# A copy moved ahead of a cast on ScalarE, and the first batch's tokens loaded in eight transfers of one head

## The chip, the core and the metric

The kernel runs on one core of a Trainium2 chip. The core has a matrix engine (TensorE, PE in the profile), three engines for elementwise work (VectorE or DVE, ScalarE or ACT, GpSimd or POOL) and a sync engine (SyncE or SP) that mostly issues DMA transfers. PE writes its products to PSUM, from which ACT or DVE copies them to SBUF; DMA moves data between main memory (HBM) and SBUF. Each engine runs its own instructions strictly in the order of the program and waits on semaphores for the others.

The metric is the device time of one execution in microseconds (us). Lower is better.

## The reference

A cross attention between 512 tokens and 32 state rows, in both directions, for 8 batches of 8 heads, then a feed-forward block over all 8 x 544 rows:

```python
def _attn_ref(x, state):                    # x (8,8,512,64), state (8,8,32,64)
    scale = 1.0 / np.sqrt(D)
    scores = scale * np.matmul(x, state.transpose(0, 1, 3, 2))
    a = softmax(scores)                     # over the 32 states
    xread = np.matmul(a, state)
    scores2 = scale * np.matmul(state, x.transpose(0, 1, 3, 2))
    a2 = softmax(scores2)                   # over the 512 tokens
    sread = np.matmul(a2, x)
    return np.concatenate([xread, sread], axis=2)

def _moe_ref(x, w_in, w_out):               # x (4352, 512): heads side by side
    h = x @ w_in                            # 512 -> 2048
    g = np.maximum(0.01 * h, h)
    return g @ w_out                        # 2048 -> 512
```

Both softmaxes subtract the maximum and add 1e-9 to the sum; they are shortened here.

## The kernel before

**Products.** For the token rows, attention and the first feed-forward product are joined: `a_m` multiplies a batch's states with `w_in` into a matrix M (2 x 128 rows, 2048 columns) in four column quarters of 512, and `ff1` multiplies the probabilities `aT` with M. So M has four quarters for each batch, each a PE product into PSUM and a copy to SBUF by `m_evict`. The second feed-forward product is `piece` for batch 0 and `Batch.run` for the later ones; the latter saves multiplications with sums of weights (`weights_sum`) and of activations.

**Order.** The program is written out by hand: `tc.manual_schedule` leaves every engine the order in which the code names its instructions. Batches overlap: while batch 0's second product runs, batch 1's scores, softmax and M are made and batch 2's tokens are cast. The steps are in the names: `a0`, `a1`, `a2` are batches 0 to 2.

**Queues.** Transfers issued by SyncE (`nc.sync`) and ScalarE (`nc.scalar`) go through one queue each, those of GpSimd (`nc.gpsimd`) through a third. The issue is itself an instruction of that engine, in order with the rest. POOL issues the weights `w_in` and `w_out`, batch 1's tokens (`x1`) and batch 2's (`load_x(2)`).

**The start.** ACT issues the states of batches 0 and 1 (`st0f`, L63). Batch 0's tokens (1 MB of float32, 8 heads) go to two tiles `xf` of four heads each, in transfers of two heads that alternate between SyncE and ScalarE (L68 to L71). Then ACT loads its function table with a warm exponential (L77) and copies the prepared states (`state01`, L164 and L168). `cast_x0` (L118) turns pairs of heads into bfloat16 in `xb`: pair 0 in one cast, pairs 1 and 2 in halves, pair 3 in halves on DVE and POOL (L883 to L889). PE transposes them (`x0_t`, L785), ACT and DVE copy the result to `xT` (`xt0_evict`, L791), and batch 0's scores follow (`scores0`, L800). Until the tokens are there PE runs products of zeros (`spin`, L142).

**Around the copy that is moved.** In this stretch (L1019 to L1048) ACT has, in order: M quarters 1 and 2 of batch 1 (`m_evict`, L388), the exponential of batch 1 (`a_exp`, L246), the cast of batch 2's first four heads (`cast_x`, L113), M quarter 3 of batch 1 (L388 again, two copies of 128x512), and the two exponentials of batch 1's other direction (`a_exp2`, L296), which read the scores in the PSUM bank `sc`. PE has: M quarter 3's product (L376), products of `piece` (L608), then batch 2's M quarter 0 (`a_m(a2, 0, "sc")`, L1070), which is written into the same bank `sc`, and batch 1's `ff1` (L397). POOL casts heads 4 to 7 of batch 2, and SyncE issues the transpose of batch 2's tokens (`a_xt_dma`, L200) once all eight heads are cast.

Of the kernel before, what the change touches and what calls it, by code (L numbers as in the profile page):

```python
# [10 lines left out]
B, H, S, D = 8, 8, 512, 64  # L11
# [5 lines left out]
NK = H // 2  # L17
# [13 lines left out]
def kernel(  # L31
# [9 lines left out]
    nc = tc.nc  # L41
# [15 lines left out]
    VEC, SCA, POO = nc.vector.tensor_copy, nc.scalar.copy, nc.gpsimd.tensor_copy  # L57
# [7 lines left out]
    )  # L65
    xf = [consts.tile([P, NK, NT * D], FP32, name="xf", tag=f"xf{u}") for u in range(2)]
    xv = x[0].rearrange("h (p t) d -> p h (t d)", t=NT)
    for k in range(NK):  # L68
        (nc.sync, nc.scalar)[k % 2].dma_start(
            xf[k // 2][:, 2 * (k % 2):2 * (k % 2) + 2], xv[:, 2 * k:2 * k + 2]  # L70
        )  # L71

    idle = consts.tile([P, S], BF16, name="idle")
    nc.vector.memset(idle[:], 0.0)
# [37 lines left out]
    def cast_x(b, h0, h1, copy):  # L112
        copy(  # L113
            xs[b][:, :, h0:h1].rearrange("p t h d -> p h t d"),
            xl[b][:, h0:h1].rearrange("p h (t d) -> p h t d", t=NT),
        )
# [68 lines left out]
    def state_t(i):  # L185
        POO(stb[i][:], stf[i][:])
        nc.sync.dma_start_transpose(st_t[i][:], stb[i][:].rearrange("p b q -> p (b q)"))
# [11 lines left out]
    def a_xt_dma(a):  # L199
        nc.sync.dma_start_transpose(  # L200
            a.xT[:].rearrange("p t k q -> p (t k) q"),
            a.xb[:].rearrange("p t h d -> p (t h d)"),
        )

    def st_of(a, g, k):
        rows = slice(D * g, D * (g + 1))
        if a.b == 0:
            return stbd[rows, k, g ^ (k // 2), :]
        t = st1 if a.b == 1 else st_t[0][:, a.b - 2] if a.b < 4 else st_t[1][:, a.b - 4]
        return t[rows, NS * k:NS * (k + 1)]  # L210
# [153 lines left out]
    def a_m(a, c, tag):  # L364
        if a.M is None:
            a.M = mpool.tile([P, 2, DFF], BF16, name="M", tag="M")
        if tag in ("ph", "py", "phpy"):
            pm = [psum.tile([P, DM], FP32, name="pm", tag=t) for t in (tag[:2], tag[-2:])]
            at = [t[:] for t in pm]
        else:  # L370
            pm = psum.tile([P, 2, DM], FP32, name="pm", tag=tag, bufs=1)
            at = [pm[:, g, :] for g in range(2)]
        for k in range(NK):
            for g in range(2):
                v, r = (k // 2, 2 * (k % 2) + (g ^ (k // 2))) if a.b == 0 else (g, k)
                nc.tensor.matmul(  # L376
                    at[v][NS * r:NS * (r + 1)],
                    lhsT=st_of(a, g, k),
                    rhs=w_in_bf[D * g:D * (g + 1), k, DM * c:DM * (c + 1)],
                    start=True, stop=True,  # L380
                )
        return pm

    def m_evict(a, c, pm, copy):
        cols = slice(DM * c, DM * (c + 1))
        if isinstance(pm, list):
            for g in range(2):
                copy(a.M[:, g, cols], pm[g][:])  # L388
        else:
            copy(a.M[:, :, cols], pm[:])  # L390
# [211 lines left out]
    def piece(b, hT, i, jq, bank=None, copy=SCA, part=range(4)):  # L602
        if jq == 0:
            y = ys[b, i] = Y()
            y.py = psum.tile([P, DM], FP32, name="py", tag="py")[:] if bank is None else bank
        y = ys[b, i]
        for j in (4 * jq + v for v in part):
            nc.tensor.matmul(  # L608
                y.py, lhsT=hT[:, j, P * i:P * (i + 1)], rhs=w_out_bf[:, j, :],
                start=(j == 0), stop=(j == 15),  # L610
            )
        if jq == 3 and copy is not None:
            y_store(b, i, copy)

    def y_store(b, i, copy):
        tag, bufs = (f"yo{i - 2}", 1) if (b, i) in ((0, 2), (0, 3)) else ("ysb", 3)
        ysb = ypool.tile([P, DM], FP32, name="ysb", tag=tag, bufs=bufs)
        copy(ysb[:], ys[b, i].py)
        if b == B:
            for bb in range(4):  # L620
                r0 = (4 * i + bb) * SROW + S
                nc.sync.dma_start(out[r0:r0 + NS, :], ysb[NS * bb:NS * (bb + 1), :])
        else:
            nc.sync.dma_start(rows_of(b)[i], ysb[:])
# [13 lines left out]
    def weights_sum(dst, m0=0, m1=NM, eng=None):  # L638
        u, v, op = (
            (B12, B11, ALU.subtract), (B11, tw[2], ALU.subtract),  # L640
            (B22, B12, ALU.add), (tw[1], B21, ALU.add),
        )[dst]
        with nc.allow_low_precision(reason="operands of a product"):
            ms = slice(m0, m1)
            (eng or nc.vector).tensor_tensor(out=tw[dst][:, ms], in0=u[:, ms], in1=v[:, ms], op=op)
# [122 lines left out]
    a0, a1, a2 = att_of[:3]  # L768
# [171 lines left out]
    h0 = hpool.tile([P, 16, S], BF16, name="hT", tag="hT")  # L940
# [67 lines left out]
    for u in range(2):  # L1008
        piece(0, h0, 1 + u, 0, bank=wide[:, 0] if u else None)
        ps = psum.tile([P, NT, 2, P], BF16, name="pxt2", tag="ph")  # L1010
        for t in range(NT):
            for v in range(2):
                h = NK * u + 2 * v
# [16 lines left out]
    weights_sum(2, 0, 4, nc.gpsimd)  # L1030
    weights_sum(1, 0, 4, nc.gpsimd)
    state_t(0)
    cast_x(2, 0, 4, SCA)
    for h in range(NK, H):
        cast_x(2, h, h + 1, POO)
    a_open(a2, 2)
    a_xt_dma(a2)
    for i in (2, 3):
        piece(0, h0, i, 1)
    m_evict(a1, 3, a_m(a1, 3, "ph"), SCA)  # L1040
    for g in range(2):
        a_exp2(a1, g)
    load_x(3, nc.sync)
# [78 lines left out]
    for b in range(2, B):  # L1122
# [16 lines left out]
        for s in range(16):  # L1139
            fast = nxt is None and 4 <= s < 12  # L1140
            if fast:
                n = 1 if s in (7, 11) else 2
                k = PACE[s]
# [192 lines left out]
```

## Time and profile before

The profile is of one execution. The table sets the figures beside each other:

| figure | value |
|---|---|
| median of 3 runs | 201.96 us (201.87 to 202.44) |
| the profiled execution's own time | 202.15 us |
| its span in the profile | 200.4 us |
| PE busy | 194.9 us, 97% of the span |
| DVE, ACT, POOL busy | 160.4, 143.6, 55.5 us |
| DMA packets | 28.01 MB, mean 140 GB/s |
| granted TensorE clock | 1.0 in the whole span |

How the profile is read. The span runs from the first to the last instruction; the execution's own time has some 1.75 us more around it. A row of the groups names line, engine and operation, what is written and read, the shape and count, the busy time with the mean length of one, and the idle time of the engine just before these instructions with what ended most of it. A row of the timeline gives the start, the time covered and the instructions, with the idle time before the first and its releaser in brackets. An engine's name with a q (ACTq, SPq) is its sequencer issuing a transfer. A matmul row is longer than the matmul's own cost, since matmuls are pipelined: the distance between starts is the better measure. The chain of waits follows the work that ended last back through what released each step; a large share there says where the time is, not what would be saved if that step were shorter.

### The profile page before, as it was taken

To read this page: it belongs to the slowest core of one execution; us is meant where nothing else is said; L and a number is where in the kernel's file an instruction comes from. 1 tells how busy PE (TensorE), PEld (TensorE's weight loads), DVE (VectorE), ACT (ScalarE), POOL (GpSimd) and SP (SyncE) were. 2 spreads that over 40 slices of the span, in tenths; PEclk is the share of its full clock that TensorE was granted. 3 is DMA by queue.
4 is the path that set the end of the run, shared out by engine and by line. 5 is a ranking of instruction groups with operands and counts; after the bars stand their busy time and mean duration, and the time that the engine had idled before them with its cause. 6 is when DMAs were issued, how large, how long until landed. Compare 5 with 4: busy or idle time off the path is not lost.

```text
span 200.4 us, 4995 instructions
## 1 busy us (share of the span) xinstructions
PE 194.9 (97%) x2066; PEld 134.6 (67%) x2066; DVE 160.4 (80%) x249; ACT 143.6 (72%) x263; POOL 55.5 (28%) x82
## 2 busy tenths in 40 slices
PE   7999999999999999999999999999999999999993
PEld 2566634346676767766776677666767788799882
DVE  2576689999999989975997499779978977995622
ACT  3388747599877867978697859787878768767710
POOL 8393174690036005200420040100020024004250
PEclk9999999999999999999999999999999999999999
DMA  6999997999672892559424844290025102310035
GB/s 184 229 207 261 241 294 130 225 292 202 143 192 53 248 264 50 98 206 258 96 39 169 270 55 89 105 164 0 0 108 157 29 0 87 125 56 0 0 95 170
DMA packets 39510, 28.01 MB, mean 140 GB/s; under 512 B 25344, under 2 KB 36736, under 8 KB 39488
## 3 DMA queue, kind: packets, MB, share of 16 engines
q1 hardware_dynamic: 33712, 20.35, 39.6%
q0 software_dynamic: 4944, 6.55, 16.0%
q10 hardware_dynamic: 832, 0.79, 1.4%
q8 instruction: 16, 0.26, 0.5%
q14 instruction: 6, 0.05, 0.1%
HBM read 17.30 MB, written 8.91 MB: 131 GB/s over the span
## 4 chain that ended last, share of the span: by engine, by line
PE 80%; DMA 14%; POOL 2%; ACT 2%; issue 0%; DVE 0%; POOLq 0%
PE yq L679 43%; PE ph L397 22%; DMA xl<-in_x_dram 8%; DMA w_in_bf<-in_moe_w_in_dram 5%; PE pf L475 3%; PE pm L376 3%; PE yu L679 3%; PE pl L564 2%; PE psn L342 1%; PE sc L216 1%; PE py L608 1%; PE phw L410 1%; POOL w_in_bf L126 1%; ACT e L296 1%; ACT xb L113 1%; ACT M L388 0%
## 5 line engine op out<-in xcount | busy, mean ns | idle before, releaser
L403 ACT ACTIVATE hT<-ph 128x512 bf16<-128x512 f32 x100 | 58.5, 605 | 17.8 <-PE ph L397 17.3
L397 PE MATMUL ph<-aT,M 128*128 128x512 bf16 x200 | 57.7, 379 | 0.0
L679 PEld LDWEIGHTS <-su 128*128 128x128 bf16 x480 | 45.9, 98 | 14.8 <-DVE su L668 0.8
L679 PEld LDWEIGHTS <-hT 128*128 128x128 bf16 x336 | 32.3, 98 | 14.3 <-issue 2.5
L679 PE MATMUL yq<-tw_xf,su 128*128 128x256 bf16 x224 | 31.5, 273 | 0.0
L679 PE MATMUL yq<-w_out_bf,hT 128*128 128x256 bf16 x224 | 31.0, 273 | 0.0
L113 POOL CAST xb<-xl 128x512 bf16<-128x512 f32 (+1 forms) x24 | 13.8, 614 | 48.4 <-DMA xl<-in_x_dram 48.4
L668 DVE TENSOR_TENSOR su<-hT 128x1024 bf16<-128x1024 bf16 (+1 forms) x27 | 18.9, 703 | 6.7 <-ACT hT L403 6.7
L397 PEld LDWEIGHTS <-M 128*128 128x128 bf16 x200 | 19.5, 98 | 5.7 <-issue 0.2
L751 POOL TENSOR_TENSOR yo<-sv,sv 128x512 f32<-128x512 f32 x7 | 9.2, 1310 | 41.0 <-issue 20.3
L688 ACT COPY sv<-yq 128x512 f32<-128x512 f32 x28 | 16.3, 585 | 3.0 <-PE yq L679 2.5
L679 PE MATMUL yq<-tw_x,su 128*128 128x256 bf16 x112 | 15.5, 273 | 0.0
L679 PE MATMUL yq<-w_out_bf,su 128*128 128x256 bf16 x112 | 15.3, 273 | 0.0
L691 DVE TENSOR_TENSOR yo<-yq,sv 128x512 f32<-128x512 f32 x20 | 13.6, 682 | 1.5 <-PE yq L679 1.5
L679 PE MATMUL yq<-tw_x,hT 128*128 128x256 bf16 x104 | 14.5, 273 | 0.0
L390 ACT CAST M<-pm 128x1024 bf16<-128x1024 f32 x12 | 12.2, 1019 | 0.2 <-PE pm L376 0.2
L296 ACT ACTIVATE e<-sc,mcols 128x512 bf16<-128x512 f32 x16 | 11.0, 694 | 0.6 <-DVE mcols L290 0.6
L608 PEld LDWEIGHTS <-hT 128*128 128x128 bf16 x64 | 5.8, 98 | 7.0 <-issue 1.1
L668 DVE TENSOR_TENSOR su<-su,hT 128x1024 bf16<-128x1024 bf16 x14 | 9.7, 692 | 0.5
L288 DVE TENSOR_REDUCE mcol<-sc 128x2 f32<-128x1024 f32 x8 | 9.7, 1215 | 0.0
L668 DVE TENSOR_TENSOR su<-hT,su 128x2048 bf16<-128x2048 bf16 (+1 forms) x8 | 9.2, 1155 | 0.0
L226 DVE TRANSPOSE_TENSOR_REDUCE mrow<-sc 128x32 f32<-128x1024 f32 x7 | 8.7, 1242 | 0.5 <-PE sc L216 0.5
(173 smaller groups left out, 303.7 us busy)
## 6 DMA issues: line engine op xcount, KB each, us to landing
out_dram<-yo SPq DMA_DIRECT2D x12, 512.0 KB, 2.8
xl<-in_x_dram SPq DMA_DIRECT2D x5, 1024.0 KB, 6.7
w_in_bf<-in_moe_w_in_dram POOLq DMA_DIRECT2D x4, 512.0 KB, 7.8
w_out_bf<-in_moe_w_out_dram POOLq DMA_DIRECT2D x2, 512.0 KB, 12.6
x<-in_x_dram POOLq DMA_DIRECT2D x2, 512.0 KB, 11.5
w_out_bf<-in_moe_w_out_dram POOLq DMA_DIRECT2D x4, 256.0 KB, 13.7
xl<-in_x_dram POOLq DMA_DIRECT2D x1, 1024.0 KB, 16.6
out_dram<-ysb SPq DMA_DIRECT2D x4, 256.0 KB, 5.6
```

The source lines that it names most:

```text
L113: copy(xs[b][:, :, h0:h1].rearrange("p t h d -> p h t d"), xl[b][:, h0:h1].rearrange("p h (t d) -> p h t d", t=NT),)
L226: nc.vector.tensor_reduce(out=m1[:], in_=flat.rearrange("p (c j) -> p c j", j=NS), axis=AX.X, op=ALU.max, apply_transpose=True,)
L288: nc.vector.tensor_reduce(out=m2[:], in_=a.sc[:], axis=AX.X, op=ALU.max, negate=True)
L296: nc.scalar.activation(out=a.e2[:, g], in_=a.sc[:, g, :], func=AF.Exp, bias=a.m2s[:, g:g + 1], scale=SCALE, accum_out=a.r2[:, g:g + 1],)
L390: copy(a.M[:, :, cols], pm[:])
L397: nc.tensor.matmul(ph[:], lhsT=a.M[:, g, P * j:P * (j + 1)], rhs=a.aT[:, g, :], start=(g == 0), stop=(g == 1),)
L403: nc.scalar.activation(out=hT[:, j, :], in_=ph[:], func=AF.Prelu, alpha=0.01)
L668: (eng or nc.vector).tensor_tensor(out=S[n][:, ms], in0=u[:, ms], in1=v[:, ms], op=op)
L679: nc.tensor.matmul(bank[:, i, :], lhsT=lhs[:, m, P * i:P * (i + 1)], rhs=rhs[:, m, :], start=(first and m == 0 and (i == 0 or of is not No ...
L688: copy(t[:], bank)
L691: nc.vector.tensor_tensor(out=dst, in0=bank, in1=self.sv[n][:], op=ALU.add)
L751: nc.gpsimd.tensor_tensor(out=self.yo(1)[:, :, HC:], in0=f.sv[7][:], in1=f.sv[5][:], op=ALU.add)
```

## The change

Two edits, both of order and grouping. Batch 0's tokens are loaded in eight transfers of one head (128 KB) instead of four of two heads, even heads issued by SyncE and odd heads by ScalarE. And the last M quarter of batch 1 (`m_evict(a1, 3, ...)`, with the PE products named before it) stands ahead of batch 2's casts instead of behind them and behind the transpose's issue. What is computed is the same.

```diff
     xv = x[0].rearrange("h (p t) d -> p h (t d)", t=NT)
-    for k in range(NK):
-        (nc.sync, nc.scalar)[k % 2].dma_start(
-            xf[k // 2][:, 2 * (k % 2):2 * (k % 2) + 2], xv[:, 2 * k:2 * k + 2]
-        )
+    for h in range(H):
+        (nc.sync, nc.scalar)[h % 2].dma_start(xf[h // NK][:, h % NK], xv[:, h])
...
     state_t(0)
+    for i in (2, 3):
+        piece(0, h0, i, 1)
+    m_evict(a1, 3, a_m(a1, 3, "ph"), SCA)
     cast_x(2, 0, 4, SCA)
     for h in range(NK, H):
         cast_x(2, h, h + 1, POO)
     a_open(a2, 2)
     a_xt_dma(a2)
-    for i in (2, 3):
-        piece(0, h0, i, 1)
-    m_evict(a1, 3, a_m(a1, 3, "ph"), SCA)
     for g in range(2):
         a_exp2(a1, g)
```

## The prediction

> **What bounds the kernel now.** I read the page first, then the chain of waits, the timelines of TensorE (PE), ScalarE (ACT) and the start, and last the windows of the DMA engines. The page gives PE 97% busy, and its two largest groups of matmuls never wait (last column, idle before them):
>
> ```profile
> L397 PE MATMUL ph<-aT,M 128*128 128x512 bf16 x200 | 57.7, 379 | 0.0
> L679 PE MATMUL yq<-tw_xf,su 128*128 128x256 bf16 x224 | 31.5, 273 | 0.0
> ```
>
> A busy PE is not a full PE, so I checked the pace: four 512-column matmuls take 0.86 us (36.88 to 37.74 in the timeline), 0.216 each, and from 19 us on starts follow each other at that pace. One place breaks it. The timeline of PE (start, length, instructions, count, idle before):
>
> ```profile
> 28.69 1.90 PE L608 MATMUL pyw<-w_out_bf,hT 128*128 128x512 bf16 x8
> 30.52 0.41 PE L376 MATMUL pm<-w_in_bf,st 64*32 64x512 bf16 x8
> 32.60 2.75 PE L608 MATMUL pyw<-w_out_bf,hT 128*128 128x512 bf16 x12
> 35.66 0.41 PE L376 MATMUL pm<-w_in_bf,st_t 64*32 64x512 bf16 x8 [0.31 <-ACT e L296]
> 36.00 1.04 PE L397 MATMUL ph<-aT,M 128*128 128x512 bf16 x4
> ```
>
> The twelve matmuls from 32.60 are through at 32.60 + 12 x 0.216 = 35.19, and the next starts at 35.66: a hole of 0.47 us. The same change from L608 to L376 costs 0.10 where nothing is waited for (28.69 + 8 x 0.216 = 30.42, next start 30.52). So 0.37 us is a wait, and the row names it: L376 wants the PSUM bank "sc", which the two exponentials of batch 1 (L296) still read. ACT at that time:
>
> ```profile
> 30.26 1.06 ACT L246 ACTIVATE e<-sh 128x1024 bf16<-128x1024 f32 x1 [0.37 <-DVE sh L239]
> 32.24 1.04 ACT L113 CAST xb<-xl 128x1024 bf16<-128x1024 f32 x1 [0.93 <-DMA xl<-in_x_dram]
> 33.20 1.06 ACT L388 CAST M<-pm 128x512 bf16<-128x512 f32 x2
> 34.15 0.70 ACT L296 ACTIVATE e<-sc,mcols 128x512 bf16<-128x512 f32 x1
> 35.39 0.22 ACT L296 ACTIVATION_READ_ACCUMULATOR e<-sc,mcols 128x1 f32 x1
> ```
>
> ACT stands still for 0.93 us waiting for batch 2's tokens, while the product that L388 copies (PE at 30.52) has been ready since 30.93. The exponentials end at 35.61, and PE starts 0.05 later.
>
> The start of the kernel, before PE is full:
>
> ```profile
> 0.74 0.42 ACTq L63 DMA_DIRECT2D st0f<-in_state_dram  x1
> 0.75 0.96 SPq L69 DMA_DIRECT2D xf<-in_x_dram  x2
> 1.19 0.98 ACTq L69 DMA_DIRECT2D xf<-in_x_dram  x2
> 2.20 1.28 ACT L77 ACT_TABLE_LOAD   x1 [2.20 <-issue]
> 3.81 0.30 DVE L772 CAST stb<-st0f 128x256 bf16<-128x256 f32 x1 [2.66 <-DMA st0f<-in_state_dram]
> 4.38 0.66 DVE L120 CAST xb<-xf 128x512 bf16<-128x512 f32 x1 [0.27 <-DMA xf<-in_x_dram]
> 6.08 1.12 DVE L120 CAST xb<-xf 128x256 bf16<-128x256 f32 x5 [1.05 <-DMA xf<-in_x_dram]
> 6.94 0.52 POOL L120 CAST xb<-xf 128x256 bf16<-128x256 f32 x1 [1.41 <-DMA xf<-in_x_dram]
> 7.12 1.50 ACT L791 COPY xT<-pxth 128x768 bf16<-128x768 bf16 x2 [1.70 <-PE pxth L785]
> 15.66 0.91 POOL L107 DMA_DIRECT2D xl<-in_x_dram  x1 [0.93 <-DMA w_in_bf<-in_moe_w_in_dram]
> ```
>
> The tile view of xf gives 3.6 to 5.1 us from issue to landing, the view of DMA issues 4.3 as SyncE's median and 5.0 as ScalarE's. With the issues at 0.75 and about 1.2 (SyncE), 1.19 and about 1.7 (ScalarE), the four pairs land at about 4.35, 6.1, 6.3 and 6.8. The five later casts run back to back from the second landing to 7.20; the transposes, ScalarE's copy at 7.12 and the first scores at 7.97 hang on them.
>
> **Part 1, the M quarter moved.** It adds and removes no instruction: two copies of 128x512 (1.06 us together) change places with one cast of 1.04 us. No PE work lies between the old place and the new, and the one transfer between them (the transpose of batch 2's tokens, SyncE) is issued in the same order on its queue. After: exponential L246 until 31.32, the copies at about 31.25 to 32.3 (the product is there at 30.93), in the 0.93 us in which ACT stood still. The cast starts at 32.25 to 32.3 instead of 32.24, at most 0.06 later. Behind it the transpose waits, but it also waits for POOL's last cast, which ends at 33.70 (32.27 + 1.43) against ACT's 33.35, so it is not late. The exponentials then start at 33.2 and end at 34.66 instead of 35.61. PE comes to L376 at 35.19 and finds the bank free: 0.47 becomes 0.10, a gain of **0.37 us**.
>
> What is late next: L376 also needs the transposed states, issued at 31.16 and landing at most 3.8 later, 34.96 (the tile view's longest of two), before 35.29. L397 then starts at 35.63; its aT ends on DVE at 34.76 + 0.69 = 35.45. L216 moves from 38.70 to 38.33; its xT lands at 33.73 + 4.3 = 38.03, and DVE frees "sc" at 36.76 + 1.22 = 37.98. Each holds, by 0.2 to 0.35. DVE is busy without a break from 36 to 44 and does not move up, so these margins are the real bound. Ends for this part: 0 (one of them gives it all back) and -0.37; I take -0.37, as every margin read is positive.
>
> **Part 2, eight transfers.** Bytes, casts and their order stay. SyncE issues 4 instead of 2 at 0.46 us, ScalarE 4 instead of 2 at 0.48, one head each, heads alternating. A cast of a pair of heads now waits for both queues. Mean DMA traffic is 363 to 383 GB/s from 3.0 to 5.5 us (windows), and their sum is 1.11 MB by 5.5; so 1.05 MB of tokens and 0.13 MB of state, moved by about 5.7, stay one stream with one end. The first pair needs the queues' first heads; it may come 0.1 to 0.3 later than 4.35, and the cover is large: PE's idle spins run to 6.0, the cast takes 0.66. The second pair, now third of the five rounds rather than filling ScalarE's queue after the state, may land about 0.4 earlier. The casts behind it are held by pairs three and four, in total bytes where they were.
>
> ScalarE's issues are the cost. The eighth head is the ninth transfer of the SyncE/ScalarE kind. POOL's queue shows what I take to be the rule here: its eleventh to thirteenth issues (15.66, and two of L134 at 17.73 and 20.28) each wait for an earlier POOL transfer to land, the third to the fifth by order, eight before. So I expect head 7's issue to wait for the state's landing, 0.74 + 3.0 = 3.74 by the view of DMA issues, DVE's cast saying 3.8. It is issued 3.85 to 4.33, and queued behind it on ACT are the table load (1.28, to 5.6), the warm exponential (0.20) and two copies (0.53, L164 and L168): done at about 6.4. Next on ACT is L791 at 7.12. The cover is 0.7 us; without it ACT's wait would go straight into the scores.
>
> No row shows such a late issue. From issue to landing the nearest rows give 3.0 (state, same size and queue) and 5.1 (the slowest token pair): head 7 lands between 6.85 and 8.95, where pair four lands at 6.8 now. I take 3.0, as the same size is asked for when the stream is nearly empty: +0.05, and with some 0.05 earlier from pairs two and three the part comes to **0.0**. Its lower end is -0.2: further up, PE's transposes of batch 1 (start 24.56) need a cast that waits for its own transfer and ends at 24.28 whatever the start does. Its upper end is +2.1. A delay there passes to the end whole, since PE is full after it.
>
> **Sum.** The profiled execution took 202.15 us, span 200.4 and 1.75 around it. -0.37 + 0.0 gives a span of 200.0 and 201.8 for that execution. It lies 0.19 above the median of the runs, 201.96; from that, **201.6**.
>
> **Rivals.**
> - *A, as summed*, 201.6, own range 201.4 to 201.8. Chance 0.57.
> - *B, the last head lands behind the weights (slower).* Place: head 7, released at about 3.8, meets the w_in transfers that POOL issues from 3.09 and that fill the engines from 5.5 (windows: 248 GB/s, then 215). For it: the 16 KB state transfers, issued from 20.15 under POOL's traffic, take 5.0 (view of DMA issues). Against it: the state's 3.0. It decides once head 7 lands after about 7.2 (6.85 plus the 0.37 of part 1); at 4.5 from issue it lands at 8.35, +1.5: 203.1. Chance 0.16.
> - *C, the tokens gain too.* Pairs two and three land earlier and the scores with them. For it: DVE idle 1.05 before the casts at 6.08. Against: the last cast needs pair four. At most -0.2 more: 201.4. Chance 0.12.
> - *D, the change does not do what it says.* The hole closes at 35.66 and opens again at aT, xT or "sc", whose margins are 0.2 to 0.35: 202.0. Chance 0.14.
> - *E, transfers of one queue follow each other.* Five of the state's 3.0 on ScalarE's queue end at 0.74 + 15 = 15.7 instead of 6.8, +8.9: 210.5. Against it: ScalarE's two pairs, issued 0.5 apart, land 0.65 apart, and pair two lands 4.9 after its issue behind the state. Chance 0.01.
>
> The Trainium skill (DMA: Bandwidth & Descriptors, Anatomy of one DMA and Rules for kernel authors) speaks against part 2: each transfer carries a fixed cost of some 2 us, small ones should be joined, and several queues share the same engines, which saves issue time only. By that rule, paid in turn, four more transfers on two queues would add 4 us and the sum would be 205.6; the 0.65 between ScalarE's landings bears out the sharing, not the paying in turn.
>
> The skill's same page (Queues, rings and completion order) says that an engine alternates between queues by packets, which would let head 7 in soon after w_in begins; by that, B's price would be a few tenths and the sum stay near 201.9. No run here shows it for these queues.
>
> **How the numbers follow.** 0.3% of 201.96 is 0.61 us, about what a measurement of this kernel can tell from no change: faster means below 201.35, slower above 202.57. A falls inside, with a little of its scatter below; C straddles the lower edge; B is above but for its near end. Faster 0.10, same 0.74, slower 0.16. The range takes A, C and D and B's near third: 201.2 to 202.8; A alone 201.4 to 201.8.
>
> **What would show it.** Part 1 is right if ACT runs L388 at about 31.3, L296 ends near 34.7 and L376 on PE starts 0.1 after the matmuls before it; wrong if PE waits there for st_t, aT or xT. Part 2 is right if the last ScalarE issue of L69 stands at about 3.85 with the table load after it, the second pair's cast starts before 6.0, POOL's cast stays near 6.9 and the first scores near 8.0. POOL's cast after 7.3 is B; scores before 7.85 are C. The prediction is wrong if the start of the scores moves by over 0.5 either way, or if PE shows a new idle place after 19 us.

## The result and the profile after

The changed kernel takes **203.21 us** (median of 7 runs, 202.49 to 203.79); the kernel before, on the same chip, 202.09 (201.70 to 202.44). The ratio is 1.0061, with a 95% interval of 1.0039 to 1.0084: slower by some 1.2 us, where 201.6 was forecast with a range up to 202.8. The profiled execution took 202.86 us with a span of 201.1, against 202.15 and 200.4: 0.7 of the loss lies in it.

Line numbers are now lower by two from line 70 on: L388 is L386, L376 is L374, L608 is L606, L120 is L118.

Still nothing interrupts the large groups on PE (the page's groups: busy us, mean ns, idle before):

```profile
L395 PE MATMUL ph<-aT,M 128*128 128x512 bf16 x200 | 57.8, 379 | 0.0
L677 PE MATMUL yq<-tw_xf,su 128*128 128x256 bf16 x224 | 31.6, 273 | 0.0
```

So the loss must be at the start, or in a slower clock. First the place that the moved copy was to mend, in the timelines of ScalarE and of PE:

```profile
31.13 1.06 ACT L244 ACTIVATE e<-sh 128x1024 bf16<-128x1024 f32 x1 [0.37 <-DVE sh L237]
32.09 1.05 ACT L386 CAST M<-pm 128x512 bf16<-128x512 f32 x2
33.03 1.06 ACT L111 CAST xb<-xl 128x1024 bf16<-128x1024 f32 x1
33.98 0.70 ACT L294 ACTIVATE e<-sc,mcols 128x512 bf16<-128x512 f32 x1
35.22 0.22 ACT L294 ACTIVATION_READ_ACCUMULATOR e<-sc,mcols 128x1 f32 x1
```

```profile
33.47 2.75 PE L606 MATMUL pyw<-w_out_bf,hT 128*128 128x512 bf16 x12
36.15 0.41 PE L374 MATMUL pm<-w_in_bf,st_t 64*32 64x512 bf16 x8
36.49 1.04 PE L395 MATMUL ph<-aT,M 128*128 128x512 bf16 x4
```

ScalarE works without a break. The twelve matmuls are through at 33.47 + 12 x 0.216 = 36.06 and the next starts at 36.15: a hole of 0.09 instead of 0.47, and its bracket "<-ACT e" is gone. But the whole row stands 0.87 later than before (33.47 against 32.60). The timeline of the start says why:

```profile
0.75 1.85 SPq L69 DMA_DIRECT2D xf<-in_x_dram  x4
...
1.16 2.71 ACTq L69 DMA_DIRECT2D xf<-in_x_dram  x4
...
3.54 0.57 DVE L770 CAST stb<-st0f 128x256 bf16<-128x256 f32 x1 [2.39 <-DMA st0f<-in_state_dram]
...
3.90 1.28 ACT L75 ACT_TABLE_LOAD   x1 [3.90 <-DMA st0f<-in_state_dram]
4.11 0.43 DVE L118 CAST xb<-xf 128x512 bf16<-128x512 f32 x1
...
5.72 0.29 DVE L118 CAST xb<-xf 128x256 bf16<-128x256 f32 x1 [1.18 <-DMA xf<-in_x_dram]
...
6.38 0.70 DVE L118 CAST xb<-xf 128x256 bf16<-128x256 f32 x3 [0.37 <-DMA xf<-in_x_dram]
...
7.54 0.29 DVE L118 CAST xb<-xf 128x256 bf16<-128x256 f32 x1 [0.47 <-DMA xf<-in_x_dram]
7.64 0.45 POOL L118 CAST xb<-xf 128x256 bf16<-128x256 f32 x1 [2.07 <-DMA xf<-in_x_dram]
...
8.27 0.61 PE L798 MATMUL sct<-stbd,xT 128*128 128x64 bf16 x8
...
10.58 0.60 ACT L848 ACTIVATE e<-scn 128x512 bf16<-128x512 f32 x1 [2.03 <-PE scn L824]
...
13.17 0.41 PE L374 MATMUL pm<-w_in_bf,stbd 64*32 64x512 bf16 x8 [0.37 <-DMA w_in_bf<-in_moe_w_in_dram]
...
16.82 0.41 PE L374 MATMUL pm<-w_in_bf,stbd 64*32 64x512 bf16 x8
```

In the kernel before, the last three of these rows stood here:

```profile
10.08 0.60 ACT L850 ACTIVATE e<-scn 128x512 bf16<-128x512 f32 x1 [1.47 <-PE scn L826]
...
12.12 0.40 PE L376 MATMUL pm<-w_in_bf,stbd 64*32 64x512 bf16 x8
...
15.96 0.41 PE L376 MATMUL pm<-w_in_bf,stbd 64*32 64x512 bf16 x8
```

Casts that ran in one piece from 6.08 to 7.20 now wait three times for tokens. The last pair's casts start at 7.54 and 7.64 (before: POOL at 6.94), the scores at 8.27 (7.97), the first exponential at 10.58 (10.08): 0.50 late. Then PE waits 0.37 more for the second transfer of `w_in`, which nothing waited for before: this product starts at 13.17 instead of 12.12. Some of it is caught up by 16.82 (before 15.96, 0.86 late). The mended hole returns 0.38 of it (0.47 less 0.09), which leaves 0.49 at the row of 36.15 (35.66), and the last PE group starts exactly 0.49 late (196.34 against 195.85). The other 0.2 of the span comes behind the last operation that the timeline shows (197.42, also 0.49 late), while the output's last transfers are landing.

The windows of the DMA engines show what happened to the stream. The columns are the stretch, its length, busy us and instructions of PE, its weight loads, DVE, ACT and POOL, then PE's clock, the DMA engines' busy share and GB/s; before first, after second:

```profile
2.00:3.00 1.00, 1.00 (x4) 0.42 (x3) 0.00 (x0) 0.80 (x1) 0.87 (x10) 1.00 0.57 133
3.00:3.50 0.50, 0.50 (x3) 0.19 (x2) 0.00 (x0) 0.49 (x2) 0.46 (x3) 1.00 1.09 383
3.50:5.50 2.00, 2.00 (x13) 0.62 (x11) 0.96 (x2) 0.74 (x3) 2.00 (x3) 1.00 1.09 373
```

```profile
2.00:3.00 1.00, 1.00 (x4) 0.42 (x3) 0.00 (x0) 0.00 (x0) 0.87 (x10) 1.00 0.95 294
3.00:3.50 0.50, 0.50 (x3) 0.18 (x2) 0.00 (x0) 0.00 (x0) 0.46 (x3) 1.00 1.03 357
3.50:5.50 2.00, 2.00 (x18) 0.75 (x15) 0.99 (x2) 1.58 (x3) 2.00 (x3) 1.00 0.90 236
```

Eight transfers move more at first (294 GB/s against 133), and then fall to 236 where four ran at 373. In these 2 us they carry 0.47 MB instead of 0.75. Summed over all windows from 0.5 to 5.5 us, 0.98 MB have been moved instead of 1.11. The busy share (above 1, packets overlap) falls less than the rate, from 1.09 to 0.90: in this stretch fewer packets are under way at a time, and a byte takes longer as well. Over the whole load it does not: added up, the packets of the states and tokens occupy the engines for 62.7 us, before for 62.5 (the traces' packet records, SyncE's and ScalarE's queues).

What the load loses shows in how a transfer ends. The trace records sixteen partial landings for each transfer, as many as the core has DMA engines, and the transfer has landed when the last of them is there. Before, the sixteen parts of the last pair land between 5.99 and 6.80. Now, of heads 3 and 4, eight parts each are there by 4.77 and 4.96, and the other eight come only from 5.45 and 5.65 on; of head 7, fifteen are there by 6.79 and the last comes at 7.52. Taken as one part for each engine, this says that some engines fall behind the others, and each cast waits for the last of them.

Last, the clock. It is 1.0 in this execution and in three of the other six. In the remaining three it is 0.992 to 0.996 on average, and these are the three longest, 203.73 to 203.79, against 202.49 to 203.21 for the four at 1.0. The kernel before had 0.996 or more in every run whose clock is on record.

### The profile page after: what moved, and what is told of

Read it like the earlier page. It is cut to its first block, busy times and chain, and to the rows that moved or that the text cites. A ratio compares the mean times of both kernels' runs of the same rounds, so it can differ in the third digit from the quotient of the medians.

```text
span 201.1 us, 5004 instructions
## 1 busy us (share of the span) xinstructions
PE 194.2 (97%) x2066; PEld 134.0 (67%) x2066; DVE 160.7 (80%) x249; ACT 143.3 (71%) x263; POOL 55.4 (28%) x82
## 4 chain that ended last, share of the span: by engine, by line
PE 92%; DMA 5%; POOL 1%; issue 0%; DVE 0%; POOLq 0%
PE yq L677 43%; PE ph L395 22%; DMA w_in_bf<-in_moe_w_in_dram 5%; PE pm L374 4%; PE py L606 4%; PE pyw L606 3%; PE pf L473 3%; PE yu L677 3%; PE ph L956 3%; PE pl L562 2%; PE sc L214 1%; PE psn L340 1%; PE php L956 1%; PE phw L408 1%; PE pxt L1012 0%; PE yz L677 0%
## 5 line engine op out<-in xcount | busy, mean ns | idle before, releaser
L666 DVE TENSOR_TENSOR su<-hT 128x1024 bf16<-128x1024 bf16 (+1 forms) x27 | 19.5, 724 | 6.7 <-ACT hT L401 6.7
L388 ACT CAST M<-pm 128x1024 bf16<-128x1024 f32 x12 | 12.2, 1019 | 0.2 <-PE pm L374 0.2
L294 ACT ACTIVATE e<-sc,mcols 128x512 bf16<-128x512 f32 x16 | 11.0, 694 | 0.6 <-DVE mcols L288 0.6
L606 PEld LDWEIGHTS <-hT 128*128 128x128 bf16 x64 | 5.8, 98 | 7.0 <-issue 1.1
L232 DVE STREAM_TRANSPOSE mrowb<-mrow 128x1024 f32<-128x1024 f32 x7 | 8.7, 1245 | 0.2
```

The source lines that it names most:

```text
L294: nc.scalar.activation(out=a.e2[:, g], in_=a.sc[:, g, :], func=AF.Exp, bias=a.m2s[:, g:g + 1], scale=SCALE, accum_out=a.r2[:, g:g + 1],)
L606: nc.tensor.matmul(y.py, lhsT=hT[:, j, P * i:P * (i + 1)], rhs=w_out_bf[:, j, :], start=(j == 0), stop=(j == 15),)
L666: (eng or nc.vector).tensor_tensor(out=S[n][:, ms], in0=u[:, ms], in1=v[:, ms], op=op)
```

## The experiments

All times are compared with the kernel before on the same chip. The cuts show the difference to the changed kernel; where only added lines are shown, they stand in place of its loop of loads. "First scores" and "last casts" are read off each kernel's profiled execution, which is one of several and not always near the median.

**The copy alone.** `e1_move_only` has the moved M quarter and loads the tokens as before.

```diff
-    for h in range(H):
-        (nc.sync, nc.scalar)[h % 2].dma_start(xf[h // NK][:, h % NK], xv[:, h])
+    for k in range(NK):
+        (nc.sync, nc.scalar)[k % 2].dma_start(
+            xf[k // 2][:, 2 * (k % 2):2 * (k % 2) + 2], xv[:, 2 * k:2 * k + 2]
+        )
```

> The M quarter moved, the tokens in four transfers of two heads as before. Theory (the loss sits in the eight transfers): the hole in PE before L376 shrinks from 0.47 to 0.10 us, the first scores stay at 7.97, the profiled span is about 200.0, and the time is 0.3 to 0.4 us under before, ratio 0.998. Rival (moving the copy itself costs, through the later cast or a margin at aT or xT): ratio 1.000 or above, with a new idle place of PE after 19 us.

Measured: 201.68 us (12 runs) against 201.94, ratio 0.9984 (0.9972 to 0.9997). Its PE timeline:

```profile
32.83 2.79 PE L608 MATMUL pyw<-w_out_bf,hT 128*128 128x512 bf16 x12
35.55 0.41 PE L376 MATMUL pm<-w_in_bf,st_t 64*32 64x512 bf16 x8
```

32.83 + 2.59 = 35.42, a hole of 0.13. The copy is worth about 0.3 us by the medians and the ratio, near the 0.37 worked out, and holds by itself. What lost the time is the other edit.

**The eight transfers alone.** `e2_split_only` leaves the M quarter where it was and has the new loop of loads.

> Eight transfers of one head, the M quarter where it was. Theory: everything from the first scores on is late as with both edits (0.5 at the first exponential, 0.9 from 16 us on), the hole before L376 stays near 0.4, and the time is 1.2 to 1.5 us over before, ratio 1.006 to 1.007. Rival (the two edits lose only together): ratio below 1.003.

Measured: 203.73 us (202.85 to 205.60), ratio 1.0091 (1.0057 to 1.0124). So splitting costs the whole loss and, within the intervals, the 0.3 that the copy returns. The profiled execution is the longest of the six, 205.6. Its timeline, and its windows with the columns as above (the clock is the third from the end):

```profile
8.61 0.29 DVE L118 CAST xb<-xf 128x256 bf16<-128x256 f32 x1 [1.65 <-DMA xf<-in_x_dram]
...
8.96 0.54 PE L783 MATMUL pxth<-ident,xb 128*128 128x128 bf16 x4 [1.66 <-DVE xb L118]
```

```profile
8.00:10.00 2.00, 0.99 (x16) 0.68 (x20) 0.96 (x4) 0.50 (x1) 0.45 (x1) 1.00 1.19 177
10.00:12.00 2.00, 1.98 (x52) 1.35 (x46) 1.16 (x4) 0.00 (x0) 1.07 (x3) 0.53 1.24 204
12.00:14.00 2.00, 1.87 (x52) 1.27 (x48) 1.40 (x5) 1.18 (x2) 2.00 (x3) 0.50 1.20 199
14.00:16.00 2.00, 2.00 (x57) 0.96 (x46) 1.18 (x2) 0.63 (x2) 2.00 (x4) 0.50 1.14 174
```

Here the last head came 5.0 us after its issue (the longest in the tile view of `xf`): thirteen of its sixteen parts were there by 6.70, the last three came at 8.22 to 8.59. PE stood still for 1.66, and about a microsecond after it started again its clock was halved for 6 us and more. That is a second price of a late token; in the changed kernel's profiled execution, whose longest gap at this place was 0.47, the clock stayed at 1.0.

**Without the wait at the last issue.** My prediction had feared the ninth transfer, whose issue waits for the states to land. `e3_six_and_pair` joins the last two heads, so that the count is again eight with the states; both edits otherwise.

```diff
-    for h in range(H):
+    for h in range(H - 2):
         (nc.sync, nc.scalar)[h % 2].dma_start(xf[h // NK][:, h % NK], xv[:, h])
+    nc.scalar.dma_start(xf[1][:, 2:4], xv[:, 6:8])
```

> Both edits, but the last two heads in one transfer of ScalarE: eight transfers of the SyncE and ScalarE kind in all, so that none waits for the state's landing. Theory 1 (the wait of the ninth transfer costs): pair four lands near 6.8 as before, the table load follows ScalarE's issues at about 2.6, the scores stand near 8.0 and the time is 0.2 to 0.4 us under before. Theory 2 (more and smaller transfers run slower, wait or no wait): heads 3 to 5 still land about 1 us apart on two groups of engines, the casts of pairs two and three are late as with both edits (5.7 and 6.4), w_in starts late, and the time lies 0.3 to 1 us over before.

Measured: 203.25 us (202.16 to 206.75, 12 runs), ratio 1.0064 (1.0040 to 1.0089), which is the changed kernel's. The profiled execution was the longest of the twelve, so the same kernel was profiled once more as `e12_six_and_pair_again`:

> The kernel with the last two heads in one transfer once more, for a second profile of it (the first was its longest execution). Theory 1 (seven token transfers slow the stream): rate from 3.5 to 5.5 us 250 to 320 GB/s, the second pair's or a later cast waits over 0.3 for tokens, POOL's cast at 7.2 or later, no wait at the last issue (table load at about 3.1), time 202.4 to 203.8. Theory 2 (the first profile was an accident): rate 350 or more, casts in one run from about 6, scores by 8.0, time under 202.2.

Measured: 203.50 us in that execution, and in its timeline:

```profile
3.10 1.28 ACT L76 ACT_TABLE_LOAD   x1 [3.10 <-issue]
...
5.85 0.29 DVE L119 CAST xb<-xf 128x256 bf16<-128x256 f32 x1 [1.22 <-DMA xf<-in_x_dram]
6.29 0.90 DVE L119 CAST xb<-xf 128x256 bf16<-128x256 f32 x4 [0.15 <-DMA xf<-in_x_dram]
6.97 0.47 POOL L119 CAST xb<-xf 128x256 bf16<-128x256 f32 x1 [1.30 <-DMA xf<-in_x_dram]
...
11.52 0.41 PE L375 MATMUL pm<-w_in_bf,stbd 64*32 64x512 bf16 x8 [1.32 <-DMA w_in_bf<-in_moe_w_in_dram]
...
14.00 0.41 PE L375 MATMUL pm<-w_in_bf,stbd 64*32 64x512 bf16 x8 [0.76 <-DMA w_in_bf<-in_moe_w_in_dram]
```

The wait is gone (the table load stands behind nothing but issues), the cost is not. It has only changed its place: the tokens are nearly in time (scores at 7.82), but the rate from 3.5 to 5.5 us is 299 GB/s, the weights come behind it, and PE waits 1.32 + 0.76 us for them. The weights' own stream is slow too: from 7 to 10 us, with all tokens landed by 6.84, it runs at 166, 151 and 157 GB/s, where the kernel before has 204 to 208. Neither theory had that: the second profile shows the slow stream of the first theory, without the late cast of POOL it expected.

**A pair that really is late.** `e4_late_pair` has four transfers, but the last pair's waits for a one-element copy on DVE into the same tile (it is overwritten by the load), which runs once the states have landed.

```diff
-    for h in range(H):
-        (nc.sync, nc.scalar)[h % 2].dma_start(xf[h // NK][:, h % NK], xv[:, h])
+    for k in range(NK - 1):
+        (nc.sync, nc.scalar)[k % 2].dma_start(
+            xf[k // 2][:, 2 * (k % 2):2 * (k % 2) + 2], xv[:, 2 * k:2 * k + 2]
+        )
...
+    nc.vector.tensor_copy(xf[1][:, 2, 0:1], st0f[:, 0, 0:1])
+    nc.scalar.dma_start(xf[1][:, 2:4], xv[:, 6:8])
     nc.scalar.activation(out=warm...
```

> The M quarter moved, four transfers of two heads, but ScalarE's second pair is held until the states have landed (a one-element copy on DVE stands between), so that it is issued at about 3.6 to 3.8 as head 7 is with both edits. Theory 1 (the late issue costs): pair four lands after 7.3, the scores come 0.4 or more late, time 0.2 us or more over before. Theory 2 (the smaller transfers cost): pair four lands by 7.0 and the time is as with the move alone, 0.2 to 0.4 under before.

Measured: 205.32 us, ratio 1.0177 (1.0150 to 1.0204).

```profile
3.77 0.39 ACTq L78 DMA_DIRECT2D xf<-in_x_dram  x1
...
9.46 0.30 DVE L122 CAST xb<-xf 128x256 bf16<-128x256 f32 x1 [3.08 <-DMA xf<-in_x_dram]
9.49 0.51 POOL L122 CAST xb<-xf 128x256 bf16<-128x256 f32 x1 [3.83 <-DMA xf<-in_x_dram]
9.81 0.54 PE L787 MATMUL pxth<-ident,xb 128*128 128x128 bf16 x4 [2.57 <-DVE xb L122]
```

Issued at 3.77, the pair lands 5.6 later: in the windows 375 to 390 GB/s until 4.5, then 66 in the half microsecond from 5.0, 139, and back to 213 and more only from 6.0. What is asked for just as the weights begin does get in between them, but slowly: from 6.0 to 8.0 us the trace has 215 packets of ScalarE's queue and 221 of the weights, one for one, a token's of 1 KB at 59 to 77 ns on average and a weight's at 96 to 105. The pair ends at 9.36, the first weights at 9.95. Part of the 3.4 us is the clock, 0.982 to 0.992 in these runs.

**The weights out of the way.** `e5_weights_behind` has both edits and lets POOL issue `w_in` only after its cast of batch 0's tokens.

```diff
-    for c in range(3):
-        load_w_in(c)
     cast_x0(0, 0, NT, VEC)
...
     cast_x0(3, 2, NT, POO)
+    for c in range(3):
+        load_w_in(c)
```

> Both edits, but POOL issues the first three w_in transfers only after its token cast. Theory 1 (POOL's weight traffic is what holds the small transfers up): heads 3 to 7 land in even steps on all engines, the last at 6.5 or before, and the casts of pairs two to four follow without gaps; the whole run is slower all the same, by 2 us or more, since w_in is late. Theory 2 (the small transfers hold each other up): the gaps between the casts of pairs two, three and four stay (0.4 us or more in at least one place) and head 7 lands after 6.8.

Measured: 208.55 us (two runs), ratio 1.0325 (1.0288 to 1.0363); PE now waits for the late weights. What was wanted is the tokens' own time:

```profile
6.15 0.29 DVE L118 CAST xb<-xf 128x256 bf16<-128x256 f32 x1 [1.50 <-DMA xf<-in_x_dram]
6.79 1.10 DVE L118 CAST xb<-xf 128x256 bf16<-128x256 f32 x4 [0.35 <-DMA xf<-in_x_dram]
...
7.25 0.50 POOL L118 CAST xb<-xf 128x256 bf16<-128x256 f32 x1 [4.09 <-DMA xf<-in_x_dram]
```

With no other transfer in the queues, the rate from 3.5 to 5.5 us is 301 GB/s, and the second pair is later still (6.15 against 5.72). Of the last head, nine of the sixteen parts are there by 5.84, and the last comes at 7.12. So the stragglers need no weights beside them. The weights probably cause part of the last head's lateness: POOL's cast starts at 7.25, against 7.64, 8.71 and 8.85 in the three executions that have the same eight transfers with the weights beside them (the changed kernel, `e2_split_only` and `e6_spin_fill`).

**Is it the clock?** `e6_spin_fill` has both edits and gives PE seven products of zeros more, to fill its gaps before the transposes of pairs two to four.

```diff
     for u, k in ((0, 0), (1, 0), (0, 1), (0, 2), (1, 1), (1, 2), (0, 3), (1, 3)):
+        if (u, k) in ((0, 1), (0, 2), (0, 3)):
+            spin(3 if k == 3 else 2, "sc")
         x0_t(u, k)
```

> Both edits, with two or three products of zeros on PE ahead of the transposes of pairs two, three and four, where PE waits. Theory (besides the late tokens, PE's waits let its clock drop to half for 3.4 or 6.8 us in a part of the runs): the granted clock is 1.0, or above 0.997, in nearly all runs, the times lie closer together than with both edits, and the ratio to before falls from 1.006 to 1.003 to 1.005. Rival (the clock plays no part): ratio 1.006 or above, clocks of 0.99 as often as before.

Measured: 203.71 us (202.79 to 203.99), ratio 1.0081 (1.0062 to 1.0099). The clock holds, at 0.998 to 1.0 in every run, and yet the time is no better. The loss does not come mainly through the clock: the changed kernel's four executions at 1.0 are 0.9 over before as well. A token that is late is late. How much of the 203.7 is the added products' own cost is not separated by this run.

**Half a step.** `e7_first_pair_split` has both edits, but splits only the first pair: five token transfers.

```diff
+    nc.sync.dma_start(xf[0][:, 0], xv[:, 0])
+    nc.scalar.dma_start(xf[0][:, 1], xv[:, 1])
+    for k in range(1, NK):
+        (nc.scalar, nc.sync)[k % 2].dma_start(
+            xf[k // 2][:, 2 * (k % 2):2 * (k % 2) + 2], xv[:, 2 * k:2 * k + 2]
+        )
```

> Both edits, but only the first pair in two transfers of one head; pairs two to four in one transfer each. Theory (the cost grows with the number of transfers): one more transfer than before, pairs two to four land within 0.2 of where they do now, ratio 0.998 to 1.001. Rival (any pair that needs both queues is late): the first cast later than 4.6 and ratio 1.003 or above.

Measured: 201.98 us (12 runs), ratio 1.0011 (0.9994 to 1.0028). One transfer more than `e1_move_only` seems to take back already what the copy gave, though the intervals just overlap.

**One queue.** `e8_one_queue` has both edits and issues all eight heads from SyncE.

> Both edits, but all eight heads issued by SyncE, ScalarE issuing the states alone. Theory 1 (two queues of small transfers get in each other's way): heads land in even steps, the stalls of 300 ns and more in ScalarE's packets are gone, ratio below 1.003. Theory 2 (small transfers are slow in themselves, and the last one is issued late on any queue): heads 6 and 7 are issued at about 3.6 and 4.1, head 7 lands after 7.0, ratio 1.006 or above.

Measured: 207.11 us, ratio 1.0261 (1.0241 to 1.0281). The last issue now stands at 4.1, its head takes up to 6.6 to land, POOL's cast starts at 10.81 and the scores at 11.45. Asked for 0.5 us later than in the changed kernel, the last head lands 3.2 later (10.69 against 7.52). Here too the clock has a part, 0.980 to 0.992.

**Fewer than four.** `e9_two_of_four` and `e10_three` have both edits with the tokens in two and in three transfers.

```diff
+    nc.sync.dma_start(xf[0][:], xv[:, 0:NK])
+    nc.scalar.dma_start(xf[1][:], xv[:, NK:H])
```

> Part 1 and batch 0's tokens in two transfers of four heads (512 KB each, one on SyncE, one on ScalarE behind the states). Theory 1 (the number of transfers sets how irregular the stream is, and the time): no landing is later than pair four's of before (about 6.8), and the cast of the first pair is later, since it now waits for four heads: it starts at about 5.2 to 5.6 instead of 4.38, still under cover; scores between 7.7 and 8.1, time 201.4 to 201.9, ratio 0.997 to 1.000, no slower than part 1 alone (0.9984). Theory 2 (four transfers of two heads are the best grain and both sides of it lose): the two tiles land together at about 6.3 to 6.8, so that all six casts (2.4 us on DVE) stand behind that and the scores start at 8.6 or later, 202.3 or more, ratio 1.002 or more.

```diff
+    nc.sync.dma_start(xf[0][:, 0:2], xv[:, 0:2])
+    nc.scalar.dma_start(xf[0][:, 2:4], xv[:, 2:4])
+    nc.sync.dma_start(xf[1][:], xv[:, NK:H])
```

> Part 1 and batch 0's tokens in three transfers: heads 0 and 1 on SyncE, heads 2 and 3 on ScalarE, heads 4 to 7 (512 KB) on SyncE. Theory 1 (fewer transfers, steadier stream): first cast at about 4.4, the last four heads land at 6.3 to 6.7, the scores start at 7.6 to 8.0, ratio 0.997 to 0.999, as part 1 alone (0.9984). Theory 2 (four transfers of two heads are the best grain): pair three, which landed before pair four, now comes with it, so DVE's casts bunch at the end; scores at 8.1 to 8.4, ratio 1.000 to 1.003.

Measured: 202.00 us, ratio 0.9998 (0.9987 to 1.0009), and 202.15 us, ratio 1.0009 (1.0000 to 1.0017). The transfers themselves are the best of all (POOL's cast at 6.44 and 6.49, no run over 202.9), as the first theory had it. But four of DVE's casts now become possible at once, at 6.33 and 6.38, and run in a row, so that the scores start no earlier (7.86 and 8.02) than with four transfers (7.80). Both theories were half right. The three-transfer kernel is behind `e1_move_only`; the two-transfer one can't be told from it.

**Cut the other way.** `e11_halves` has both edits and again eight transfers of 128 KB, but each holds half the partitions of a pair instead of a single head.

```diff
+    for k in range(NK):
+        for g in range(2):
+            (nc.sync, nc.scalar)[g].dma_start(
+                xf[k // 2][64 * g:64 * g + 64, 2 * (k % 2):2 * (k % 2) + 2],
+                xv[64 * g:64 * g + 64, 2 * k:2 * k + 2],
+            )
```

> Both edits with eight token transfers of 128 KB, cut another way: each pair of heads in two transfers of 64 partitions, the lower half issued by SyncE and the upper by ScalarE. Theory 1 (the number of transfers in flight and the late ninth issue set the cost, however the data is cut): rate from 3.5 to 5.5 us 230 to 320 GB/s, POOL's cast at 7.4 or later, scores at 8.2 or later, time 203.0 or more, ratio 1.005 or more. Theory 2 (the cost comes from where the data of single heads lies, or from which engines a transfer of all 128 partitions is spread over): rate 340 or more, POOL's cast by 7.0, scores by 8.0, ratio 0.997 to 1.002.

Measured: 204.96 us (204.11 to 207.00, 6 runs), ratio 1.0139 (1.0110 to 1.0168), with 276 GB/s and the scores at 11.28 in the profiled execution, its longest. The first theory: it is not a matter of single heads and where they lie; eight pieces are slow cut this way too, and slower. The last piece was issued at 3.2, earlier than in the changed kernel, and ended at 10.47, with twelve of its sixteen parts there by 7.19: the late issue alone does not make a piece late.

**All together**, by number of token transfers. The fourth column has the first and the last of the sixteen partial landings of the last token transfer, the fifth the time from issue to landing of the first `w_in` transfer; the rows are of one execution each, the ratios of all runs; the row of seven is `e12_six_and_pair_again` with the ratio of `e3_six_and_pair`, whose own profile, its longest execution, has 270 GB/s, 5.71 to 7.27, 8.9, 7.40 and 8.23:

| kernel | token transfers | GB/s, 3.5 to 5.5 us | last tokens, us | first w_in, us | POOL's cast, us | first scores, us | ratio to before |
|---|---|---|---|---|---|---|---|
| e9_two_of_four | 2 | 361 | 5.72 to 6.31 | 5.8 | 6.44 | 7.86 | 0.9998 |
| e10_three | 3 | 372 | 5.80 to 6.36 | 6.3 | 6.49 | 8.02 | 1.0009 |
| before | 4 | 373 | 5.99 to 6.80 | 6.1 | 6.94 | 7.97 | 1 |
| e1_move_only | 4 | 352 | 5.72 to 6.51 | 5.9 | 6.65 | 7.80 | 0.9984 |
| e7_first_pair_split | 5 | 333 | 5.54 to 6.58 | 6.0 | 6.71 | 7.94 | 1.0011 |
| e3 and e12, six and a pair | 7 | 299 | 5.78 to 6.84 | 8.4 | 6.97 | 7.82 | 1.0064 |
| changed kernel | 8 | 236 | 5.78 to 7.52 | 7.5 | 7.64 | 8.27 | 1.0061 |
| e6_spin_fill | 8 | 253 | 7.15 to 8.73 | 6.4 | 8.85 | 9.47 | 1.0081 |
| e2_split_only | 8 | 314 | 5.70 to 8.59 | 8.2 | 8.71 | 9.34 | 1.0091 |
| e11_halves | 8, by partitions | 276 | 6.34 to 10.47 | 9.5 | 10.59 | 11.28 | 1.0139 |
| e4_late_pair | 4, one held | 277 | 8.22 to 9.36 | 6.9 | 9.49 | 10.18 | 1.0177 |
| e8_one_queue | 8, one queue | 235 | 8.18 to 10.69 | 8.9 | 10.81 | 11.45 | 1.0261 |
| e5_weights_behind | 8, weights later | 301 | 5.69 to 7.12 | 5.6 | 7.25 | 8.32 | 1.0325 |

The rate in this stretch is lower with each kernel of five transfers or more, but it does not order the kernels by itself: those that start faster have less left to move. By 5.5 us `e2_split_only` and `e5_weights_behind` have moved 1.10 MB, as much as the kernel before (1.11), and their last tokens are late all the same. What grows is the distance between the first and the last part: 0.6 to 0.8 us with two to four transfers (none held), 1.0 to 1.6 with five and seven, 1.4 to 4.1 with eight. The loss is paid in the last tokens, in the weights, or in both. `e1_move_only` is the best version that was run.

## Why the prediction was wrong

**What bounds the kernel: right.** PE is full after 19 us; no new idle place came up there, and the last PE group moved by exactly what the row at 36.15 had moved.

**Part 1: right, in mechanism and size.** The copies start right behind the exponential, L294 is done at 35.44, and the hole is 0.09 where 0.10 was forecast; alone the edit gave 0.3 of the 0.37. The margins behind it were close, as written: in `e1_move_only` aT is ready at 35.83 and its reader L397 starts at 35.89. Rival D did not come about.

**Part 2: the step that failed** is the sentence that tokens and states "stay one stream with one end", in total bytes where they were. By it and by the size of head 7 part 2 was put at 0.0; in the profiled execution it cost 0.87 (the row at 33.47 against 32.60). Bytes did stay; the rate did not, 236 GB/s instead of 373 from 3.5 to 5.5 us, and the stream had no one end: the last transfer's parts ended 1.74 us apart instead of 0.81. I had read the rate of a stream of five transfers off the windows and used it for nine. The second wrong size is head 7: taken as 3.0 us from issue to landing, because the state took 3.0. By the rows it took 4.0 (from the issue at 3.54, in ScalarE's timeline, to the cast at 7.54), and up to 5.0 in `e2_split_only`. The state had been first on empty engines; head 7 came ninth, issued 0.45 after the first of the weights. I had written down 5.1, a pair's, as the other bound; that row was farther off in size, but nearer in what stood ahead of it. The sign set for being wrong, a start of the scores that moves by over 0.5, did not show it: they began 0.30 late. Their second part, for which the last pair has to be copied (DVE's L789 at 8.21, before L791 at 7.58), was 0.51 late (9.28 against 8.77).

**A term was missing:** the weights, which come behind the tokens on the same engines. Their transfers landed 8.7 us after issue instead of 7.8 (the medians of the page's DMA issues), and PE waited 0.37 for one of them; in `e12_six_and_pair_again` that term was 2.1, more than its whole loss (203.50 against 202.01). And the price of a long gap in the clock was in none of the cases. The three executions with a lowered clock are about 0.8 longer (203.75 against 202.94, averages); that the clock alone makes this difference is not shown, since those executions have no trace.

**The wait at the ninth issue: right, and beside the point.** The last issue stands at 3.54, when the states landed, with the table load behind it at 3.90 and not at 2.20 (forecast: 3.85 at the earliest for the issue):

```profile
3.54 0.33 ACTq L69 DMA_DIRECT2D xf<-in_x_dram  x1
```

The cover held: ScalarE was done with its copies at 5.83, and L789 came at 7.05 for other reasons. `e3_six_and_pair` takes the wait away and costs the same.

**The rivals.** By the test laid down for it, POOL's cast after 7.3 (it was 7.64), B happened, and its 203.1 is close to the 203.2 measured. That closeness is luck in good part: B had head 7 landing at 8.35 and the whole 1.5 lost there, while it landed at 7.52 and delayed the first exponential by 0.50; the weights and the clock, which B did not price, made up the rest. Its mechanism is a part of the cause. `e4_late_pair` and `e8_one_queue` show it best: what is asked for late has to share the engines with the weights. But `e5_weights_behind` shows the stream ragged without any weights, and `e3_six_and_pair` without the late issue; B named neither, nor the weights as what is late. C had one thing right, the second pair's cast came 0.36 earlier (5.72), and it was worth nothing since the last pair was late. E is far off. B's chance of 0.16 was too low: the rows of the pairs (up to 5.1) and of the small state transfers (5.0) spoke for it, one row, of 3.0, against it.

The Trainium skill (DMA: Bandwidth & Descriptors, Rules for kernel authors), which says to join small transfers, pointed the right way: the table above agrees down to four. The 2 us for each, which the Trainium skill gives for transfers issued by GpSimd (Anatomy of one DMA) and which would have made 205.6, was not paid in turn: from `e1_move_only` to the changed kernel, four transfers more, the ratio rises by 0.0077, 1.6 us or 0.4 each. The Trainium skill's account of queues that alternate by packets (DMA: Bandwidth & Descriptors, Queues, rings and completion order) agrees with the one for one of `e4_late_pair`. The price of a few tenths that I drew from it does not: that kernel paid 3.4 us.

**What stays open:** why, with more transfers, some parts fall so far behind the others. The traces do not name the engine of a part. The packets' total time is the same (62.7 and 62.5 us), the weights are not needed for it (`e5_weights_behind`), `e11_halves` speaks against the heads' place in memory, and no run tells the queue's own work for each transfer from the order in which the queues are served. Nor is it shown why the loss falls on the tokens in one kernel and on the weights in another, and why the weights of `e12_six_and_pair_again` run slowly with no token left.

## What to carry to other kernels

Moving an operation into an idle stretch of its engine, with each margin behind it read off the timeline, could be forecast here to a tenth of a microsecond. Cutting a load into more transfers can't be costed by bytes: measure the stream with the new number in flight, ask when the last part of each transfer lands and not how many bytes have moved, and price the last piece by a transfer that was issued as late and behind as many others, not by one of the same size. Split only as far as the consumer needs to start early, here four pieces: fewer bunch the casts, with more the last parts come late.

## What the runs showed of the hardware

- The same megabyte of tokens, cut into more transfers, ran at a lower rate from 3.5 to 5.5 us, in one execution each: 352 to 373 GB/s with two to four (none held), 333 with five, 270 and 299 with seven, 235 to 314 with eight. With seven or eight the first of the weights' transfers behind it landed 6.4 to 9.5 us after its issue, with two to five (none held) 5.8 to 6.3.
- A transfer's sixteen partial landings spread further with more transfers: those of the last tokens over 0.59 us in `e9_two_of_four`, 0.81 before, 1.74 in the changed kernel and 2.89 in `e2_split_only`, where three parts of sixteen came 1.5 us and more after the other thirteen.
- The ninth transfer of SyncE and ScalarE together was not issued before the first had landed: in the changed kernel at 3.54, when DVE's cast of the states starts too; with eight transfers in all there was no such wait.
- A pair asked for at 3.77, 0.7 after the weights' first issue (3.09), landed 5.6 us later, where the pairs asked for earlier in the same execution took 3.4 to 4.3. From 6.0 to 8.0 us its packets and the weights' went one for one (215 and 221).
- After a gap of 1.66 us on PE in `e2_split_only`, the granted clock was 0.50 to 0.53 from 10 to 16 us and 1.0 again from 18; with the gaps filled by products of zeros it stayed at 0.998 or above in all runs.
